# A tanh-shrink polynomial in factored form, its squares and mask on ScalarE, and a shorter weight conversion, in an mLSTM and feed-forward kernel on one core

## The chip, the cores and the metric

One Trainium2 chip, one of its cores. The metric is the device time of one launch in microseconds, as the median of several runs. Engines: TensorE multiplies matrices (PE in the profile, its weight load PEld), VectorE (DVE) and GpSimd (POOL) work elementwise, ScalarE (ACT) evaluates functions, SyncE (SP) issues the loads.

## The reference, cut to what matters

```python
for t in range(S):                                   # q, k, v: (4, 8, 768, 40)
    m_new = np.maximum(f_gate[:, :, t] + m, i_gate[:, :, t])
    f_stab = np.exp(f_gate[:, :, t] + m - m_new); i_stab = np.exp(i_gate[:, :, t] - m_new)
    C = f_stab * C + i_stab * outer(v_t, k_t)
    n = f_stab * n + i_stab * k_t
    y[:, :, t] = sigmoid(o_gate[:, :, t]) * (C @ q_t) / np.maximum(np.abs(n . q_t), 1.0)
...
h = x @ w_in              # x: y as 3072 tokens x 320; w_in: 320 x 2048, float64
g = h - np.tanh(h)        # the "shrink"
out = g @ w_out           # w_out: 2048 x 320, float64
```

Both weight matrices arrive as float64 and the result is float32.

## The kernel before

**Two halves, interleaved.** The recurrence is worked in 24 cell units (6 chunks of 128 tokens for each of 4 batches, 8 heads at once): matmuls for the decay `pd`, the scores `ps`, the products `ph`, `pi`, `pc`, with elementwise work between. Two units make a token group of 256 tokens, transposed into `xT`. The feed-forward part runs over 12 groups g and 8 pairs p of 128-row slices of the 2048 hidden features. For each (g, p), `up` makes six matmuls into one PSUM tile `ph_up` (128 x 512), `shrink` turns it into `gt` in SBUF, and two pairs later (LAG = 2) `down` makes four matmuls with `w_out` into `po`. `ph_up` has two buffers in turn.

**The shrink.** `h - tanh(h)` loses its digits for small h. So for h*h up to 0.1225 (`SMALL`) an odd polynomial in h stands in for it: a degree-9 one in four coefficients (`POLY`) with z = h*h. ScalarE copies h out of PSUM, squares it into z and takes Tanh; GpSimd makes t = h - tanh(h); VectorE makes four polynomial steps into `gt`, a compare of z with `SMALL` in place, and a predicated copy of t over `gt` where z is large (L384 to L394).

**The weights.** `weights` (L167) turns a float64 block into float32 from its two 32-bit words, `hi` and `lo`. It cuts exponent `w_e`, upper mantissa `w_m` and lower mantissa `w_r` out of the words on VectorE (L182, L183, L186, L187), rescales the three on ScalarE (L184, L188, L189), adds and multiplies them on GpSimd (L190, L191) and merges the sign on VectorE (L192). There are 40 blocks: three of `w_in` (128, 128 and 64 rows by 256 columns) and two of `w_out` (128 x 320) for each p. The loads go through four `w64` buffers; `w_e`, `w_m` and `w_r` have two each. Blocks of the first three p are converted beside the first four cell units, the other five p within the first token group, three pairs ahead of their use (EARLY = 3).

**What sets the order.** The code lists work by rough costs and merges cell work with dense work; the tile framework then sets each engine's order and its waits. In the trace every engine works its queue strictly in that order.

Of the kernel before, what the change touches and what calls it, by code (L numbers as in the profile page):

```python
# [25 lines left out]
FP = mybir.dt.float32  # L26
BF = mybir.dt.bfloat16
I32 = mybir.dt.int32
I64 = mybir.dt.int64
AF = mybir.ActivationFunctionType  # L30
OP = mybir.AluOpType
PSUM = bass.MemoryType.PSUM
# [1 line left out]
L = 128  # L34


POLY = (0.333333319193414, -0.13332963338892476, 0.05381595747274004, -0.019838061344260048)
SMALL = 0.35 * 0.35


# [1 line left out]
def kernel(  # L42
# [14 lines left out]
    V, A, G, T = nc.vector, nc.scalar, nc.gpsimd, nc.tensor  # L57

    B, NT, D, H, _ = qT.shape
# [8 lines left out]
    TG = GT * L  # L68
# [3 lines left out]
    LAG = 2  # L72

    const = ctx.enter_context(tc.tile_pool(name="const", bufs=1))
# [3 lines left out]
    mlp = ctx.enter_context(tc.tile_pool(name="mlp", bufs=2))  # L78
# [34 lines left out]
    after = const.tile([128, 128], FP, name="after")  # L113
    bar = const.tile([128, 128], BF, name="bar")
    ones = const.tile([128, D], FP, name="ones")
    make_identity(nc, ident)
    make_identity(nc, ident_b)
    V.memset(ones, 1.0)
# [27 lines left out]
    def to_columns(row):  # L146
        p = ps_b.tile([L, NT, BH], FP, name="pcol", tag="b")
        for c in range(NT):
            T.transpose(p[:, c, :], row[:, c * L:(c + 1) * L], ident[0:BH, 0:BH])
        return p  # L150

    V.tensor_copy(out=lfT, in_=to_columns(lf))
    A.activation(out=eiT, in_=to_columns(i_sb), func=AF.Exp)
    for dst, w in ((eG, upto), (eS, after), (eT, ones)):
        p = ps_b.tile([dst.shape[0], NT, BH], FP, name="psum_lf", tag="b")
        T.matmul(p.rearrange("p c n -> p (c n)"), w, lfT.rearrange("p c n -> p (c n)"),
                 start=True, stop=True)
        A.activation(out=dst, in_=p, func=AF.Exp)

# [7 lines left out]
    def weights(dst, src):  # L167

        p, n = dst.shape
        if src.dtype == FP:  # L170
            nc.sync.dma_start(out=dst, in_=src)
            return
        st = conv.tile([128, n], I64, name="w64", tag="w64", bufs=4)[0:p]
        nc.sync.dma_start(out=st, in_=src)
        words = st.bitcast(I32).rearrange("p (n two) -> p n two", two=2)
        lo, hi = words[:, :, 0], words[:, :, 1]
        e = conv.tile([128, n], I32, name="w_e", tag="w_e")[0:p]
        m = conv.tile([128, n], I32, name="w_m", tag="w_m")[0:p]
        r = conv.tile([128, n], I32, name="w_r", tag="w_r")[0:p]
        mf, rf = m.bitcast(FP), r.bitcast(FP)  # L180

        V.tensor_scalar(out=e, in0=hi, scalar1=20, scalar2=0x7FF, op0=OP.logical_shift_right, op1=OP.bitwise_and)  # L182
        V.tensor_scalar(out=e, in0=e, scalar1=896.0, scalar2=1151.0, op0=OP.max, op1=OP.min)  # L183
        A.activation(out=e, in_=e, func=AF.Copy, scale=float(1 << 23), bias=-896.0 * (1 << 23))  # L184

        V.tensor_single_scalar(m, hi, 0xFFFFF, op=OP.bitwise_and)  # L186
        V.tensor_single_scalar(r, lo, 8, op=OP.logical_shift_right)  # L187
        A.activation(out=mf, in_=m, func=AF.Copy, scale=2.0 ** -20, bias=1.0)  # L188
        A.activation(out=rf, in_=r, func=AF.Copy, scale=2.0 ** -44)  # L189
        G.tensor_tensor(out=rf, in0=rf, in1=mf, op=OP.add)  # L190
        G.tensor_tensor(out=rf, in0=rf, in1=e.bitcast(FP), op=OP.mult)  # L191
        V.scalar_tensor_tensor(out=dst.bitcast(I32), in0=hi, scalar=-(1 << 31), in1=r,  # L192
                               op0=OP.bitwise_and, op1=OP.bitwise_or)
# [3 lines left out]
    def load_w_in(j):  # L197
        cols = slice(j * WB, (j + 1) * WB)
        for c, (r0, rows) in enumerate(KC):
            weights(w_in[0:rows, c, cols], moe_w_in[r0:r0 + rows, cols])  # L200

    def load_w_out(f):
        weights(w_out[:, f, :], moe_w_out[f * 128:(f + 1) * 128, :])
# [31 lines left out]
    def scores(n, half):  # L235
        h4 = slice(half * HH, (half + 1) * HH)

        def decay():
# [6 lines left out]
            t["E"] = att.tile([L, HH, L], FP, name="E", tag="E")  # L245
            A.activation(out=t["E"], in_=pd, func=AF.Exp)  # L246

# [115 lines left out]


    gT, po = {}, {}
    c0, c1, c2, c3 = POLY

    def up(g, p):
        ph = {}

        def product(i, j):
            if not ph:
                ph[0] = ps_h.tile([128, 2, TG], FP, name="ph_up", tag="ph")
            f = 2 * p + i
            T.matmul(ph[0][:, i, :], w_in[:, j, f * 128:(f + 1) * 128], xT[g % 2][:, j, :],  # L375
                     start=(j == 0), stop=(j == NK - 1))
            if (i, j) == (1, NK - 1):
                shrink(ph[0])

        def shrink(ph):  # L380
            h = mlp.tile([128, 2, TG], FP, name="h", tag="h")
            z = mlp.tile([128, 2, TG], FP, name="z", tag="z")
            t = mlp.tile([128, 2, TG], FP, name="t", tag="t")
            A.copy(out=h, in_=ph)  # L384
            A.activation(out=z, in_=ph, func=AF.Square)  # L385
            A.activation(out=t, in_=ph, func=AF.Tanh)  # L386
            G.tensor_tensor(out=t, in0=h, in1=t, op=OP.subtract)  # L387
            gt = gT[g, p] = mlp.tile([128, 2, TG], FP, name="gt", tag="gt", bufs=LAG + 2)
            V.scalar_tensor_tensor(out=gt, in0=z, scalar=c2 / c3, in1=z, op0=OP.add, op1=OP.mult)  # L389
            V.scalar_tensor_tensor(out=gt, in0=gt, scalar=c1 / c3, in1=z, op0=OP.add, op1=OP.mult)  # L390
            V.scalar_tensor_tensor(out=gt, in0=gt, scalar=c0 / c3, in1=z, op0=OP.add, op1=OP.mult)  # L391
            V.scalar_tensor_tensor(out=gt, in0=gt, scalar=c3, in1=h, op0=OP.mult, op1=OP.mult)  # L392
            V.tensor_single_scalar(z, z, SMALL, op=OP.is_gt)  # L393
            V.copy_predicated(gt, z.bitcast(I32), t)  # L394

        return [(0.43, lambda i=i, j=j: product(i, j)) for i in range(2) for j in range(NK)]

# [38 lines left out]
    for x in range(len(pairs) + LAG):  # L436
        g, p = divmod(x, NP)
# [55 lines left out]
```

## Time and profile before

| | |
|---|---|
| median of 3 runs | 795.27 us (794.84 to 796.79) |
| profiled execution | 795.82 us, span 794.1 us |
| TensorE matmul busy | 714.1 us, 90% of the span |
| VectorE busy | 701.9 us, 88%, 1093 instructions |
| ScalarE busy | 249.9 us, 31%, 533 instructions |
| GpSimd busy | 341.5 us, 43%, 333 instructions |
| DMA | 34.93 MB, mean 44 GB/s |

Busy time is the time between an instruction's start and end, so it holds what an instruction waits inside itself. "Idle before, releaser" at a row's end is what the engine waited for ahead of it. The span runs from the first to the last instruction; some 1.7 us of the execution's time lie around it.

### The profile page before, as it was taken

The page shows a single profiled execution, that of the slowest core. Times are in us where ns is not written, and L with a number is a line of the kernel's source. Part 1 is how long each engine was busy: PE and PEld are TensorE (multiplying, and loading weights), DVE is VectorE, ACT ScalarE, POOL GpSimd, SP SyncE. Part 2 cuts the span into 40 slices and gives each one's busy share as a digit, 9 for nine tenths or more (in the row PEclk, how much of TensorE's full clock was granted, in tenths as well). Part 3 has the DMA queues.
Part 4 walks back from the last instruction along what each step waited for, and adds up shares of the span by engine and source line. Part 5 has one row for each costly group of instructions (what it writes and reads, how often), then busy time and mean ns, then how long its engine had stood idle before and what let it go on. Part 6 is the DMA issues. An engine that isn't in the chain of part 4 may idle for free.

```text
span 794.1 us, 10022 instructions
## 1 busy us (share of the span) xinstructions
PE 714.1 (90%) x3562; PEld 549.0 (69%) x3562; DVE 701.9 (88%) x1093; ACT 249.9 (31%) x533; POOL 341.5 (43%) x333
## 2 busy tenths in 40 slices
PE   4655947559999999999999999999999999999996
PEld 2433635327778778777777877877877888787784
DVE  8888887888999889889889889888988998889996
ACT  1442443432322332223223222323223233323332
POOL 7766847664344443433433433433333332222331
PEclk9856996768999999999999999999999999999999
DMA  5344222210110110101111111002101000000000
GB/s 159 92 133 134 82 74 84 75 50 9 51 34 26 41 34 26 50 26 38 38 34 43 34 26 51 26 25 59 42 26 35 24 9 17 1 17 1 0 18 17
DMA packets 21618, 34.93 MB, mean 44 GB/s; under 512 B 2688, under 2 KB 14976, under 8 KB 21568
## 3 DMA queue, kind: packets, MB, share of 16 engines
q1 hardware_dynamic: 18112, 30.35, 13.4%
q10 hardware_dynamic: 3456, 3.93, 1.3%
q8 instruction: 28, 0.46, 0.3%
q14 instruction: 22, 0.18, 0.1%
HBM read 30.34 MB, written 3.93 MB: 43 GB/s over the span
## 4 chain that ended last, share of the span: by engine, by line
PE 61%; DVE 22%; POOL 8%; issue 6%; ACT 2%; DMA 0%; ACTq 0%; DVEq 0%; POOLq 0%
PE ph_up L375 23%; PE po L403 20%; PE ps L253 4%; PE pd L244 4%; POOL w_r L190 3%; PE ph L305 3%; DVE gt L390 3%; POOL w_r L191 2%; PE pi L274 2%; DVE gt L389 2%; DVE gt L392 2%; DVE gt L391 2%; DVE gt L394 2%; PE pc L285 2%; DVE z L393 2%
## 5 line engine op out<-in xcount | busy, mean ns | idle before, releaser
L375 PE MATMUL ph_up<-xT,w_in 128*128 128x256 f32 x1152 | 332.9, 404 | 20.8 <-DVE w_in L192 18.9
L403 PE MATMUL po<-w_out,gt 128*128 128x320 f32 x768 | 269.4, 461 | 9.5 <-DVE gt L394 9.1
L387 POOL TENSOR_TENSOR t<-h,t 128x512 f32<-128x512 f32 x96 | 136.0, 1416 | 295.9 <-ACT t L386 285.6
L375 PEld LDWEIGHTS ph_up<-xT,w_in 128*128 128x128 f32 x1152 | 200.3, 196 | 59.6 <-issue 22.1
L403 PEld LDWEIGHTS po<-w_out,gt 128*128 128x128 f32 x768 | 132.2, 196 | 35.0 <-DVE gt L394 10.8
L384 ACT COPY h<-ph_up 128x512 f32<-128x512 f32 x96 | 56.1, 584 | 223.9 <-PE ph_up L375 141.5
L390 DVE SCALAR_TENSOR_TENSOR gt<-gt,z 128x512 f32<-128x512 f32 x96 | 121.3, 1264 | 2.3
L389 DVE SCALAR_TENSOR_TENSOR gt<-z 128x512 f32<-128x512 f32 x96 | 83.6, 871 | 41.6 <-ACT z L385 41.6
L253 PEld LDWEIGHTS ps<-qT,kT 128*128 128x128 f32 x384 | 69.5, 207 | 36.7 <-ACT E L246 13.8
L253 PE MATMUL ps<-qT,kT 128*128 128x128 f32 x384 | 72.3, 295 | 10.2 <-ACT E L246 6.2
L305 PEld LDWEIGHTS ph<-vw,P 128*128 128x128 f32 x384 | 67.8, 193 | 17.3 <-DVE state L290 1.8
L394 DVE COPY_PREDICATED gt<-z,t 128x512 f32<-128x512 int32 x96 | 75.7, 789 | 2.8
L391 DVE SCALAR_TENSOR_TENSOR gt<-gt,z 128x512 f32<-128x512 f32 x96 | 73.1, 762 | 2.2
L392 DVE SCALAR_TENSOR_TENSOR gt<-gt,h 128x512 f32<-128x512 f32 x96 | 72.3, 753 | 1.3
L274 PEld LDWEIGHTS pi<-state,qT 128*128 128x128 f32 x320 | 61.1, 195 | 17.7 <-ACT xT L343 3.8
L225 POOL TENSOR_TENSOR Vt<-lfT,upto 128x1024 f32<-128x1024 f32 x24 | 46.3, 1929 | 33.2 <-PE pd L244 21.8
L385 ACT ACTIVATE z<-ph_up 128x512 f32<-128x512 f32 x96 | 57.8, 602 | 7.4 <-DVE gt L394 7.4
L305 PE MATMUL ph<-vw,P 128*128 128x41 f32 x384 | 57.5, 249 | 1.4 <-DVE state L290 1.4
L386 ACT ACTIVATE t<-ph_up 128x512 f32<-128x512 f32 x96 | 57.7, 601 | 0.0
L244 PE MATMUL pd<-Vt,after 128*128 128x512 f32 x96 | 54.8, 655 | 0.0
L190 POOL TENSOR_TENSOR w_r<-w_r,w_m 128x256 f32<-128x256 f32 (+2 forms) x40 | 38.3, 957 | 35.7 <-ACT w_r L189 35.7
L274 PE MATMUL pi<-state,qT 128*128 128x41 f32 x320 | 50.6, 245 | 2.9 <-ACT xT L343 2.9
(82 smaller groups left out, 698.0 us busy)
## 6 DMA issues: line engine op xcount, KB each, us to landing
w<-in_moe_w_out SPq DMA_DIRECT2D x16, 320.0 KB
w<-in_moe_w_in SPq DMA_DIRECT2D x16, 256.0 KB
qT<-in_qT SPq DMA_DIRECT2D x24, 160.0 KB
kT<-in_kT SPq DMA_DIRECT2D x24, 160.0 KB
v<-in_v SPq DMA_DIRECT2D x24, 160.0 KB
k<-in_k SPq DMA_DIRECT2D x24, 160.0 KB
o<-in_o_gate SPq DMA_DIRECT2D x24, 160.0 KB
out<-ob ACTq DMA_DIRECT2D x24, 160.0 KB
```

What stands on the lines that cost most here:

```text
L244: T.matmul(pd, after, t["Vt"][:, h4, :], start=False, stop=True)
L253: T.matmul(t["ps"][:, j, :], t["kT"][:, h, :], t["qT"][:, h, :], start=True, stop=True)
L274: T.matmul(t["pi"][:, h, :], t["qT"][:, h, :], old[:, h, :], start=True, stop=True)
L305: T.matmul(t["ph"][:, h, :], t["P"][:, h, :], t["vw"][:, h, :], start=True, stop=True)
L375: T.matmul(ph[0][:, i, :], w_in[:, j, f * 128:(f + 1) * 128], xT[g % 2][:, j, :], start=(j == 0), stop=(j == NK - 1))
L387: G.tensor_tensor(out=t, in0=h, in1=t, op=OP.subtract)
L389: V.scalar_tensor_tensor(out=gt, in0=z, scalar=c2 / c3, in1=z, op0=OP.add, op1=OP.mult)
L390: V.scalar_tensor_tensor(out=gt, in0=gt, scalar=c1 / c3, in1=z, op0=OP.add, op1=OP.mult)
L391: V.scalar_tensor_tensor(out=gt, in0=gt, scalar=c0 / c3, in1=z, op0=OP.add, op1=OP.mult)
L392: V.scalar_tensor_tensor(out=gt, in0=gt, scalar=c3, in1=h, op0=OP.mult, op1=OP.mult)
L394: V.copy_predicated(gt, z.bitcast(I32), t)
L403: T.matmul(po[tt], gT[g, p][:, i, tt * L:(tt + 1) * L], w_out[:, f, :], start=(f == 0), stop=(f == NFF - 1))
```

## The change

The polynomial is written as lead * (z + root) * ((z + c)^2 + rest) * h * z. ScalarE gives z, Tanh, q = (z + c)^2 as a Square with a bias, and the mask `big` as Relu(z - SMALL). VectorE reads h straight from PSUM, in w = (h * lead) * z and in t = h - tanh(h), and no copy of h is made. GpSimd has no part in the shrink. For the weights VectorE masks the exponent bits, shifts the upper mantissa left, and merges the sign; ScalarE rescales, clamps the exponent from below by Relu, and reads the low words itself. GpSimd's two products stay.

```diff
+    V.memset(rebias, -896.0 * (1 << 23))
+    V.memset(square, POLY[2])
+    V.memset(border, -SMALL)
...
-        lo, hi = words[:, :, 0], words[:, :, 1]
+        lo, hi = st.bitcast(U32).rearrange("p (n two) -> p n two", two=2)[:, :, 0], words[:, :, 1]
...
-        V.tensor_scalar(out=e, in0=hi, scalar1=20, scalar2=0x7FF, op0=OP.logical_shift_right, op1=OP.bitwise_and)
-        V.tensor_scalar(out=e, in0=e, scalar1=896.0, scalar2=1151.0, op0=OP.max, op1=OP.min)
-        A.activation(out=e, in_=e, func=AF.Copy, scale=float(1 << 23), bias=-896.0 * (1 << 23))
-
-        V.tensor_single_scalar(m, hi, 0xFFFFF, op=OP.bitwise_and)
-        V.tensor_single_scalar(r, lo, 8, op=OP.logical_shift_right)
-        A.activation(out=mf, in_=m, func=AF.Copy, scale=2.0 ** -20, bias=1.0)
-        A.activation(out=rf, in_=r, func=AF.Copy, scale=2.0 ** -44)
+        V.tensor_single_scalar(e, hi, 0x7FF00000, op=OP.bitwise_and)
+        A.activation(out=e, in_=e, func=AF.Relu, scale=8.0, bias=rebias[0:p])
+
+        V.tensor_single_scalar(m, hi, 12, op=OP.logical_shift_left)
+        A.activation(out=mf, in_=m.bitcast(U32), func=AF.Copy, scale=2.0 ** -32, bias=1.0)
+        A.activation(out=rf, in_=lo, func=AF.Copy, scale=2.0 ** -52)
         G.tensor_tensor(out=rf, in0=rf, in1=mf, op=OP.add)
         G.tensor_tensor(out=rf, in0=rf, in1=e.bitcast(FP), op=OP.mult)
...
-            A.copy(out=h, in_=ph)
             A.activation(out=z, in_=ph, func=AF.Square)
             A.activation(out=t, in_=ph, func=AF.Tanh)
-            G.tensor_tensor(out=t, in0=h, in1=t, op=OP.subtract)
...
-            V.scalar_tensor_tensor(out=gt, in0=z, scalar=c2 / c3, in1=z, op0=OP.add, op1=OP.mult)
-            V.scalar_tensor_tensor(out=gt, in0=gt, scalar=c1 / c3, in1=z, op0=OP.add, op1=OP.mult)
-            V.scalar_tensor_tensor(out=gt, in0=gt, scalar=c0 / c3, in1=z, op0=OP.add, op1=OP.mult)
-            V.scalar_tensor_tensor(out=gt, in0=gt, scalar=c3, in1=h, op0=OP.mult, op1=OP.mult)
-            V.tensor_single_scalar(z, z, SMALL, op=OP.is_gt)
-            V.copy_predicated(gt, z.bitcast(I32), t)
+            A.activation(out=q, in_=z, func=AF.Square, bias=square)
+            A.activation(out=big, in_=z, func=AF.Relu, bias=border)
+            V.scalar_tensor_tensor(out=w, in0=ph, scalar=lead, in1=z, op0=OP.mult, op1=OP.mult)
+            V.tensor_tensor(out=t, in0=ph, in1=t, op=OP.subtract)
+            V.scalar_tensor_tensor(out=w, in0=z, scalar=root, in1=w, op0=OP.add, op1=OP.mult)
+            V.scalar_tensor_tensor(out=gt, in0=q, scalar=rest, in1=w, op0=OP.add, op1=OP.mult)
+            V.copy_predicated(gt, big.bitcast(I32), t)
```

The line numbers grow by 5 to 6 in the changed code (L182 becomes L189, L192 becomes L197, L375 becomes L380). VectorE's order where the first blocks of the seventh pair's weights are converted (a number behind a name marks the buffer: w64_1027, w64_1042 and w64_1057 are the pair's three w_in blocks), before:

```order
L182 TENSOR_SCALAR w_e_1029<-w64_1027 128x256
L394 COPY_PREDICATED gt_1008<-z_1002,t_1003 128x512
L183 TENSOR_SCALAR w_e_1029<-w_e_1029 128x256
L186 TENSOR_SCALAR w_m_1030<-w64_1027 128x256
L187 TENSOR_SCALAR w_r_1031<-w64_1027 128x256
L182 TENSOR_SCALAR w_e_1044<-w64_1042 128x256
L186 TENSOR_SCALAR w_m_1045<-w64_1042 128x256
L183 TENSOR_SCALAR w_e_1044<-w_e_1044 128x256
L187 TENSOR_SCALAR w_r_1046<-w64_1042 128x256
L389 SCALAR_TENSOR_TENSOR gt_1121<-z_1115 128x512
L186 TENSOR_SCALAR w_m_1060<-w64_1057 64x256
L390 SCALAR_TENSOR_TENSOR gt_1121<-gt_1121,z_1115 128x512
```

and now, with w64_976 and w64_989 as its first two:

```order
L192 TENSOR_SCALAR w_m_979<-w64_976 128x256
L396 SCALAR_TENSOR_TENSOR w_1057<-ph_up_1041,z_1053 128x512
L197 SCALAR_TENSOR_TENSOR w_out_173<-w64_905,w_r_909 128x320
L197 SCALAR_TENSOR_TENSOR w_out_173<-w64_918,w_r_922 128x320
L189 TENSOR_SCALAR w_e_978<-w64_976 128x256
L189 TENSOR_SCALAR w_e_991<-w64_989 128x256
L192 TENSOR_SCALAR w_m_992<-w64_989 128x256
L397 TENSOR_TENSOR t_1055<-ph_up_1041,t_1055 128x512
L398 SCALAR_TENSOR_TENSOR w_1057<-z_1053,w_1057 128x512
L197 SCALAR_TENSOR_TENSOR w_in_172<-w64_976,w_r_980 128x256
L399 SCALAR_TENSOR_TENSOR gt_1058<-q_1054,w_1057 128x512
L197 SCALAR_TENSOR_TENSOR w_in_172<-w64_989,w_r_993 128x256
```

Two steps a block instead of four stand ahead of the merges, and the subtraction t stands among them. ScalarE's order at the same place, before:

```order
L385 ACTIVATE z_1248<-ph_up_1219 128x512
L184 ACTIVATE w_e_1029<-w_e_1029 128x256
L188 ACTIVATE w_m_1030<-w_m_1030 128x256
L189 ACTIVATE w_r_1031<-w_r_1031 128x256
L184 ACTIVATE w_e_1044<-w_e_1044 128x256
L188 ACTIVATE w_m_1045<-w_m_1045 128x256
L189 ACTIVATE w_r_1046<-w_r_1046 128x256
L188 ACTIVATE w_m_1060<-w_m_1060 64x256
L386 ACTIVATE t_1249<-ph_up_1219 128x512
L184 ACTIVATE w_e_1059<-w_e_1059 64x256
```

and now:

```order
L392 ACTIVATE z_1177<-ph_up_1149 128x512
L193 ACTIVATE w_m_979<-w_m_979 128x256
L393 ACTIVATE t_1179<-ph_up_1149 128x512
L194 ACTIVATE w_r_980<-w64_976 128x256
L194 ACTIVATE w_r_993<-w64_989 128x256
L190 ACTIVATE w_e_978<-w_e_978,rebias_112 128x256
L190 ACTIVATE w_e_991<-w_e_991,rebias_112 128x256
L193 ACTIVATE w_m_992<-w_m_992 128x256
L394 ACTIVATE q_1178<-z_1177,square_113 128x512
L395 ACTIVATE big_1180<-z_1177,border_114 128x512
L194 ACTIVATE w_r_1006<-w64_1002 64x256
```

The low words' activations come first and read the loaded block, and q and big stand ahead of the next block's.

More of the change, by code (lines that the diff above doesn't have):

```diff
@@ L29 @@
 I64 = mybir.dt.int64
+U32 = mybir.dt.uint32
 AF = mybir.ActivationFunctionType
@@ L34 @@
 L = 128
-POLY = (0.333333319193414, -0.13332963338892476, 0.05381595747274004, -0.019838061344260048)
+POLY = (-0.019838061344260048, -2.6070109206805303, -0.05287600604508702, 6.442407825412434)
 SMALL = 0.35 * 0.35
@@ L115 @@
     ones = const.tile([128, D], FP, name="ones")
+    rebias = const.tile([128, 1], FP, name="rebias")
+    square = const.tile([128, 1], FP, name="square")
+    border = const.tile([128, 1], FP, name="border")
+    V.memset(rebias, -896.0 * (1 << 23))
+    V.memset(square, POLY[2])
+    V.memset(border, -SMALL)
     make_identity(nc, ident)
@@ L365 @@
     gT, po = {}, {}
-    c0, c1, c2, c3 = POLY
+    lead, root, _, rest = POLY
     def up(g, p):
@@ L380, in shrink @@
         def shrink(ph):
-            h = mlp.tile([128, 2, TG], FP, name="h", tag="h")
             z = mlp.tile([128, 2, TG], FP, name="z", tag="z")
+            q = mlp.tile([128, 2, TG], FP, name="q", tag="q")
             t = mlp.tile([128, 2, TG], FP, name="t", tag="t")
-            A.copy(out=h, in_=ph)
+            big = mlp.tile([128, 2, TG], FP, name="big", tag="big")
+            w = mlp.tile([128, 2, TG], FP, name="w", tag="w")
+            gt = gT[g, p] = mlp.tile([128, 2, TG], FP, name="gt", tag="gt", bufs=LAG + 2)
             A.activation(out=z, in_=ph, func=AF.Square)
             A.activation(out=t, in_=ph, func=AF.Tanh)
-            G.tensor_tensor(out=t, in0=h, in1=t, op=OP.subtract)
-            gt = gT[g, p] = mlp.tile([128, 2, TG], FP, name="gt", tag="gt", bufs=LAG + 2)
-            V.scalar_tensor_tensor(out=gt, in0=z, scalar=c2 / c3, in1=z, op0=OP.add, op1=OP.mult)
-            V.scalar_tensor_tensor(out=gt, in0=gt, scalar=c1 / c3, in1=z, op0=OP.add, op1=OP.mult)
-            V.scalar_tensor_tensor(out=gt, in0=gt, scalar=c0 / c3, in1=z, op0=OP.add, op1=OP.mult)
-            V.scalar_tensor_tensor(out=gt, in0=gt, scalar=c3, in1=h, op0=OP.mult, op1=OP.mult)
-            V.tensor_single_scalar(z, z, SMALL, op=OP.is_gt)
-            V.copy_predicated(gt, z.bitcast(I32), t)
+            A.activation(out=q, in_=z, func=AF.Square, bias=square)
[5 more added lines that the diff above has]
+            V.copy_predicated(gt, big.bitcast(I32), t)
         return [(0.43, lambda i=i, j=j: product(i, j)) for i in range(2) for j in range(NK)]
```

## The prediction

> **What bounds the kernel now.** I read the busy time by stretches first, then the chain of waits, then single rows of the timeline. Columns of the stretches: from:to, length, then busy us (x instructions) of TensorE matmul, weight load, VectorE, ScalarE and GpSimd, the granted TensorE clock, DMA share, GB/s.
>
> ```profile
> 13.00:100.00 87.00, 60.47 (x288) 42.13 (x287) 74.84 (x144) 34.69 (x88) 64.12 (x73) 0.76 0.36 107
> 100.00:174.00 74.00, 44.68 (x149) 30.23 (x150) 60.37 (x132) 29.90 (x76) 48.85 (x49) 0.76 0.26 76
> 174.00:188.00 14.00, 10.62 (x39) 7.25 (x38) 11.73 (x18) 2.85 (x6) 4.55 (x4) 0.57 0.00 1
> 188.00:720.00 532.00, 530.13 (x2801) 416.53 (x2801) 480.33 (x702) 158.82 (x319) 197.30 (x170) 1.00 0.11 31
> 720.00:780.00 60.00, 59.16 (x255) 47.23 (x255) 56.87 (x78) 19.90 (x39) 17.23 (x12) 1.00 0.02 6
> 780.00:794.10 14.10, 7.28 (x26) 4.30 (x24) 7.68 (x11) 2.43 (x5) 1.54 (x1) 0.98 0.06 23
> ```
>
> From 188 to 780 us TensorE has work in 589.3 of 592 us at full clock. VectorE is 90% busy there, but nobody waits for it: relief of VectorE in that stretch is worth at most the 2.7 us that TensorE idles. What can move are the first 188 us and the last 14.
>
> In the first stretch the weights are converted. TensorE's rows (start, length) show each of the first token group's later up-projections ending with matmuls that waited for the last converted w_in block:
>
> ```profile
> 115.39 1.99 PE L375 MATMUL ph_up<-xT,w_in 128*128 128x256 f32 x8 [2.83 <-DVE w_in L192]
> 134.10 3.78 PE L375 MATMUL ph_up<-xT,w_in 128*128 128x256 f32 x8 [1.56 <-DVE w_in L192]
> 153.84 3.78 PE L375 MATMUL ph_up<-xT,w_in 128*128 128x256 f32 x8 [3.72 <-DVE w_in L192]
> 170.35 3.78 PE L375 MATMUL ph_up<-xT,w_in 128*128 128x256 f32 x8 [0.64 <-DVE w_in L192]
> 188.02 2.40 PE L375 MATMUL ph_up<-xT,w_in 128*128 128x256 f32 x10
> ```
>
> They end at 117.4, 137.9, 157.6 and 174.1 us: 18.9 us an iteration (five weight blocks, one shrink, a quarter of a cell unit), against 6.7 us an iteration later (592 us over 88). The second group starts at 188.0. If conversion ends sooner by some time, everything after it starts sooner by as much.
>
> What holds conversion is seen in VectorE and GpSimd rows side by side:
>
> ```profile
> 106.39 1.43 POOL L191 TENSOR_TENSOR w_r<-w_r,w_e 128x256 f32<-128x256 f32 x1
> 106.56 0.68 DVE L390 SCALAR_TENSOR_TENSOR gt<-gt,z 128x512 f32<-128x512 f32 x1
> 107.78 0.72 POOL L190 TENSOR_TENSOR w_r<-w_r,w_m 128x256 f32<-128x256 f32 x1
> 108.71 0.81 DVE L182 TENSOR_SCALAR w_e<-w 64x256 int32<-64x256 int32 x1
> 109.33 1.31 POOL L387 TENSOR_TENSOR t<-h,t 128x512 f32<-128x512 f32 x1
> 109.44 1.48 DVE L192 SCALAR_TENSOR_TENSOR w_in<-w,w_r 128x256 int32<-128x256 int32 x1
> ...
> 104.03 0.28 DVE L187 TENSOR_SCALAR w_r<-w 128x256 int32<-128x256 int32 x1
> 104.23 0.28 DVE L182 TENSOR_SCALAR w_e<-w 128x256 int32<-128x256 int32 x1
> 110.84 0.28 DVE L183 TENSOR_SCALAR w_e<-w_e 64x256 int32<-64x256 int32 x1
> 29.60 0.41 DVE L192 SCALAR_TENSOR_TENSOR w_in<-w,w_r 64x256 int32<-64x256 int32 x1
> ...
> 67.28 0.31 DVE L182 TENSOR_SCALAR w_e<-w 128x320 int32<-128x320 int32 x1
> 67.51 0.31 DVE L186 TENSOR_SCALAR w_m<-w 128x320 int32<-128x320 int32 x1
> ...
> 126.06 0.86 POOL L191 TENSOR_TENSOR w_r<-w_r,w_e 128x256 f32<-128x256 f32 x1
> 126.26 0.41 DVE L340 COPY xT<-px 128x256 f32<-128x256 f32 x1
> ...
> L225 POOL TENSOR_TENSOR Vt<-lfT,upto 128x1024 f32<-128x1024 f32 x24 | 46.3, 1929 | 33.2 <-PE pd L244 21.8 <-DVE lfT L152 4.6 <-DVE gt L394 4.5
> ```
>
> With GpSimd idle, a conversion step starts 0.20 us after the one before (0.23 for 320 columns); beside a GpSimd operation it takes 0.81. A GpSimd product of 0.72 takes 1.43 when a VectorE operation came first. So the two engines take turns on SBUF operands; their busy times hold each other's waits twice and can't be read as work. The copy from PSUM at 126.26 ran through beside GpSimd. Check of the turns: a record overlaps the next by 0.08, so an iteration's free turns are GpSimd 9.1 (products of five blocks 6 x 0.72 + 4 x 0.86 = 7.8, t 1.3) and VectorE 9.5 (20 conversion steps 4.3, five merges 1.8, shrink 3.4), and by my estimate 2 for the quarter of a cell unit (Vt alone takes 1.9 a unit). The sum, 20.6, is close to the measured 18.9, so about 0.92 of a turn is path.
>
> **The change part by part.** Columns of the next rows: stretch, length, VectorE busy (x), clock, DMA; in order L182, L183, L186, L187. Below them groups: busy, mean ns.
>
> ```profile
> 0.00:188.00 188.00, 23.31 (x40) 0.76 0.32 93
> 0.00:188.00 188.00, 13.86 (x40) 0.76 0.32 93
> 0.00:188.00 188.00, 17.81 (x40) 0.76 0.32 93
> 0.00:188.00 188.00, 17.98 (x40) 0.76 0.32 93
> ...
> L393 DVE TENSOR_SCALAR z<-z 128x512 f32<-128x512 f32 x96 | 44.1, 459 | 0.0
> L394 DVE COPY_PREDICATED gt<-z,t 128x512 f32<-128x512 int32 x96 | 75.7, 789 | 2.8
> L255 DVE TENSOR_TENSOR P<-ps,E 128x512 f32<-128x512 f32 x48 | 32.6, 680 | 0.0
> L385 ACT ACTIVATE z<-ph_up 128x512 f32<-128x512 f32 x96 | 57.8, 602 | 7.4 <-DVE gt L394 7.4
> ```
>
> Conversion: four single-input steps a block become two (mask, shift), the merge stays. Two steps fewer are 24 x 0.41 + 16 x 0.47 = 17.4 us of turns over 40 blocks. The least this can be worth is nothing (hidden behind GpSimd), the most is the difference in busy time, 73.0 - 40 x 2 x 0.45 = 37 us; I take the turns, since rows free of waits measure them. ScalarE reads the low words itself, every second word; no row shows ScalarE with such a step. VectorE's stepped L187 takes 0.28 like the dense L183, so I take 0.41 as now; at double, 40 x 0.41 = 16 us more lie on ScalarE, 40% busy before 188 us. The first ScalarE operation then waits for the DMA alone.
>
> Shrink: out go the ScalarE copy h, two VectorE steps (one short: L393) and GpSimd's t, in come a ScalarE square and Relu (2 x 0.60, less the copy's 0.58: 0.6 us more) and a subtraction on VectorE, five operations for six. Free turns before: 4 x 0.60 + 0.34 + 0.65 = 3.4 on VectorE plus 1.3 on GpSimd. After: w and t read PSUM, priced by L255 (0.68, no dearer than an SBUF one), and like L340 they should wait for no GpSimd operation; the other three hold 2 x 0.60 + 0.65 = 1.85. So 2.85 us of turns a shrink, 20 us over the seven before 188 us. If PSUM sources took turns too, it is 7 x 1.2 = 8 us less.
> The Trainium skill (SBUF — State Buffer, "Who interferes with whom") says the lock is exclusive and that a VectorE instruction with at most one SBUF input, outside the two-port modes, doesn't contend with GpSimd. That speaks for the first price; L340's row agrees only in part, since it has no SBUF input at all, and no run yet shows w's and t's form. By the rule the sum stays; against it, 768.
>
> The ACT queue: q and big stand ahead of later blocks' activations. At 8 x 0.6 us and 40% busy that is covered by ScalarE's idle time; uncovered, 5 us. The ph_up buffer is now freed by VectorE's subtraction instead of ScalarE's Tanh (a rival below). SP's queue keeps its steps; w64 buffers are still freed by the merge, so loads come earlier with it: 107 GB/s in the first stretch would have to become about 130, below the 157 GB/s of the first 20 us:
>
> ```profile
> 0.00:20.00 20.00, 8.52 (x38) 5.67 (x39) 16.86 (x22) 4.04 (x10) 14.67 (x33) 1.00 0.55 157
> ...
> 780.12 2.32 PE L403 MATMUL po<-w_out,gt 128*128 128x320 f32 x8
> 784.20 2.42 PE L403 MATMUL po<-w_out,gt 128*128 128x320 f32 x8 [1.76 <-DVE gt L394]
> 788.11 2.42 PE L403 MATMUL po<-w_out,gt 128*128 128x320 f32 x8 [1.49 <-DVE gt L394]
> ```
>
> The end: TensorE waits 1.76 + 1.49 for the last two shrinks. After the last up-projection (780.3) the new chain is z, Tanh, then t, w, gt, predicated copy: 1.2 + 4 x 0.65 = 3.8, ready at 784.2; the two earlier down-projections run to 784.4. Both waits go: -3.3 us.
>
> Sum: conversion after 81 us, 25 blocks, 10.9 and shrinks 20, times 0.92: 28.4; the first 15 blocks, 6.5 of turns, half of it path, because cell work and waits for ScalarE share that stretch: 3.3; the end 3.3. Together 35. The profiled execution took 795.8 (span 794.1 and 1.7 around), the median is 795.3: 760.
>
> **The rivals.**
> *The busy time comes off whole.* 37 us of conversion, 9.2 of GpSimd's t (seven times 1.31), the end 3.3: 49.5, so 746. For it: VectorE is 85% busy in the stretch. Against: the turns counted twice.
> *The chain hardly shortens.* The chain of waits from 117.4 to 174.1 us:
>
> ```profile
> by line: POOL w_r L190 18.1%; issue 16.6%; POOL w_r L191 13.7%; DVE w_e L182 10.9%; DVE w_in L192 6.9%; ACT w_e L184 6.1%; DVE w_m L186 5.2%; ACT w_r L189 5.0%; DVE w_e L183 4.0%; DVE z L393 2.5%; DVE gt L394 2.4%; DVE w_out L192 2.3%; ACT
> ```
>
> GpSimd's two products lead it and stay. Only L182 and L183, 14.9% of 56.7 us, go: 2.8 an iteration, 14 over five groups of blocks, and the end: 778. The other steps' waits would then take the place of the removed ones.
> *Slower.* VectorE now frees ph_up. The next use of a buffer is two iterations on; from 720 to 780 us, with hardly any cell work, an iteration (12 + 8 matmul records, of 255 in 60 us) takes 4.7 us, its up-projection some 2.6, so 6.8 us pass between the end of one and the reuse. With VectorE's queue more than that behind, TensorE stalls in each of 88 iterations: at 0.5 us each 44 us, over the 35 gained: 804. Against: five operations of 0.7 fit into 4.7 us.
> *No change.* Something else, such as loads, sets the end of conversion: 795.
>
> **How the numbers follow.** A difference under 0.3% can't be told from none. The sum of turns (750 to 770): 0.59. Busy time whole (740 to 750): 0.17. Chain hardly shorter (770 to 785): 0.17. No change: 0.03. Slower: 0.04. Faster 0.93, same 0.03, slower 0.04. The range reaches to the two priced neighbours, 743 to 779, which leaves out under 2 in 10.
>
> **What would show it.** Second group's first up-projection near 156 instead of 188 us; iterations near 14 us between the waits for w_in; GpSimd products nearer 0.72 and 0.86; the two waits at the end gone; 188 to 780 unchanged in length. Wrong if TensorE then waits for the subtraction, or if w and t take over 1 us beside GpSimd, or if ScalarE's reads of low words take 0.8.

## The result, and the profile after

The changed kernel takes 761.66 us (median; 761.25 to 762.04) against 795.19 us (794.84 to 796.79): a ratio of 0.9575, 95% interval 0.9558 to 0.9591, 33.5 us less. The forecast was 760 us. The sum held; two of its terms were wrong by 6 and 13 us in opposite directions, and a third of nearly 6 us was missing. The runs below separate them. Single executions of one kernel differ by up to 3.6 us, so a stretch read from one profiled execution can lie up to 2.8 us from what the medians give.

The stretches of the changed kernel, cut at the first group's first up-projection, the second group's first one, and the end of the last one (columns as in the prediction: from:to, length, busy us of TensorE matmul, weight load, VectorE, ScalarE, GpSimd, then clock and DMA), and the same cuts of before:

```profile
0.00:77.80 77.80, 48.95 (x225) 33.20 (x225) 58.11 (x97) 29.99 (x71) 58.01 (x83) 0.77 0.43 129
77.80:162.79 84.99, 65.45 (x270) 47.49 (x270) 71.92 (x132) 50.81 (x112) 54.76 (x61) 0.81 0.29 88
162.79:749.40 586.61, 586.61 (x3049) 462.59 (x3048) 415.69 (x688) 242.19 (x442) 93.83 (x94) 1.00 0.10 29
749.40:760.30 10.90, 6.85 (x25) 4.25 (x23) 3.36 (x6) 3.15 (x6) 0.00 (x0) 0.96 0.09 30
```
```profile
0.00:81.25 81.25, 45.77 (x223) 31.50 (x223) 69.37 (x127) 27.61 (x70) 57.08 (x81) 0.77 0.44 128
81.25:188.02 106.77, 71.79 (x266) 49.43 (x265) 87.71 (x178) 41.13 (x101) 68.32 (x70) 0.76 0.22 67
188.02:780.30 592.28, 589.57 (x3056) 464.02 (x3056) 537.48 (x780) 178.70 (x358) 214.53 (x182) 1.00 0.10 29
780.30:794.10 13.80, 6.98 (x24) 4.03 (x23) 7.38 (x11) 2.43 (x5) 1.54 (x1) 0.98 0.06 24
```

The four stretches give back 3.5, 21.8, 5.7 and 2.9 us: 33.8 of the span. In the second stretch VectorE is still the busy engine (85%; in the first it is as busy as GpSimd, 58.1 and 58.0 us); in the third TensorE now shows no idle time at all. The up-projections of the first group, as TensorE's rows show them, no longer end with matmuls that wait for a converted block; three of them start with one that waits for VectorE's subtraction to free `ph_up`, two of these shown:

```profile
113.22 3.30 PE L380 MATMUL ph_up<-xT,w_in 128*128 128x256 f32 x12
126.75 5.09 PE L380 MATMUL ph_up<-xT,w_in 128*128 128x256 f32 x12 [5.21 <-DVE t L397]
141.95 4.33 PE L380 MATMUL ph_up<-xT,w_in 128*128 128x256 f32 x12 [5.81 <-DVE t L397]
162.79 2.84 PE L380 MATMUL ph_up<-xT,w_in 128*128 128x256 f32 x12
...
754.24 2.42 PE L409 MATMUL po<-w_out,gt 128*128 128x320 f32 x8 [0.42 <-DVE gt L400]
```

The last row is the end: of the two waits for the last shrinks one is left, 0.42 us. VectorE and GpSimd side by side:

```profile
119.72 1.89 POOL L230 TENSOR_TENSOR Vt<-lfT,upto 128x1024 f32<-128x1024 f32 x1
119.79 1.97 DVE L192 TENSOR_SCALAR w_m<-w 128x256 int32<-128x256 int32 x1 [0.72 <-POOL w_r L195]
121.57 0.91 POOL L196 TENSOR_TENSOR w_r<-w_r,w_e 128x320 f32<-128x320 f32 x1
121.68 0.68 DVE L396 SCALAR_TENSOR_TENSOR w<-ph_up,z 128x512 f32<-128x512 f32 x1
...
112.20 0.77 POOL L195 TENSOR_TENSOR w_r<-w_r,w_m 128x256 f32<-128x256 f32 x1
112.31 0.68 DVE L397 TENSOR_TENSOR t<-ph_up,t 128x512 f32<-128x512 f32 x1
```

A shift that takes 0.28 us alone is 1.97 us long when GpSimd's `Vt` came first. `w` and `t`, which read one operand from PSUM, take 0.68 us beside a GpSimd operation, and none of their 96 records each is over 0.70. The Trainium skill ("SBUF — State Buffer", "Who interferes with whom": no contention with at most one SBUF input outside the two-port modes) agrees with the two rows. The prediction said that no run showed this form yet; L255 of before has it (`ps` in PSUM, `E` in SBUF), and its 48 records there lie between 0.67 and 0.69 us.

Groups of VectorE in the second stretch (busy, mean ns, idle before), then of GpSimd in the first 163 us, then of ScalarE over the whole span:

```profile
L192 DVE TENSOR_SCALAR w_m<-w 128x320 int32<-128x320 int32 (+2 forms) x23 | 12.3, 534 | 0.9 <-POOL w_r L195 0.9
L197 DVE SCALAR_TENSOR_TENSOR w_in<-w,w_r 128x256 int32<-128x256 int32 (+1 forms) x15 | 9.9, 659 | 7.5 <-POOL w_r L196 7.5
L189 DVE TENSOR_SCALAR w_e<-w 128x320 int32<-128x320 int32 (+2 forms) x23 | 9.9, 432 | 0.0
L197 DVE SCALAR_TENSOR_TENSOR w_out<-w,w_r 128x320 int32<-128x320 int32 x10 | 7.7, 768 | 4.6 <-POOL w_r L196 4.6
...
L195 POOL TENSOR_TENSOR w_r<-w_r,w_m 128x256 f32<-128x256 f32 (+2 forms) x40 | 36.0, 900 | 24.5 <-ACT w_m L193 21.9 <-ACT w_r L194 2.3
L196 POOL TENSOR_TENSOR w_r<-w_r,w_e 128x256 f32<-128x256 f32 (+2 forms) x40 | 34.4, 860 | 5.2 <-ACT w_e L190 2.6
...
L394 ACT ACTIVATE q<-z,square 128x512 f32<-128x512 f32 x96 | 69.3, 722 | 0.0
L395 ACT ACTIVATE big<-z,border 128x512 f32<-128x512 f32 x96 | 69.1, 719 | 0.0
L392 ACT ACTIVATE z<-ph_up 128x512 f32<-128x512 f32 x96 | 57.2, 596 | 208.0 <-PE ph_up L380 206.0 <-DMA out<-ob 1.8
L190 ACT ACTIVATE w_e<-w_e,rebias 128x256 int32<-128x256 int32 (+2 forms) x40 | 20.9, 524 | 13.9 <-DVE w_e L189 13.8
L193 ACT ACTIVATE w_m<-w_m 128x256 f32<-128x256 uint32 (+2 forms) x40 | 17.2, 430 | 9.3 <-DVE w_m L192 9.1
L194 ACT ACTIVATE w_r<-w 128x256 f32<-128x256 uint32 (+2 forms) x40 | 18.1, 452 | 21.3 <-DVE w_out L197 10.9 <-DVE w_in L197 10.1
```

The steps that stay are still long, 0.43 to 0.77 us on average, and VectorE idles 13.0 us there for GpSimd's products.

### The profile page after: what moved, and what is told of

Its sections match the earlier page's. It is cut to its first block, busy times and chain, and to the rows that moved or that the text cites. A ratio compares the mean times of both kernels' runs of the same rounds, so it can differ in the third digit from the quotient of the medians.

```text
span 760.3 us, 9877 instructions
## 1 busy us (share of the span) xinstructions
PE 707.9 (93%) x3562; PEld 547.5 (72%) x3562; DVE 549.1 (72%) x920; ACT 326.1 (43%) x629; POOL 206.6 (27%) x237
## 3 DMA queue, kind: packets, MB, share of 16 engines
q1 hardware_dynamic: 18112, 30.35, 13.5%
## 4 chain that ended last, share of the span: by engine, by line
PE 78%; POOL 10%; DVE 6%; issue 4%; ACT 2%; ACTq 0%; POOLq 0%; DVEq 0%
PE ph_up L380 33%; PE po L409 27%; PE ps L258 4%; PE pd L249 4%; PE ph L310 3%; POOL w_r L195 3%; PE pi L279 3%; POOL w_r L196 3%; PE pc L290 2%; PE px L341 1%; POOL Vt L230 1%; DVE w_m L192 1%; PE pd L248 1%; DVE w_e L189 1%; DVE w_in L197 1%
## 5 line engine op out<-in xcount | busy, mean ns | idle before, releaser
L380 PE MATMUL ph_up<-xT,w_in 128*128 128x256 f32 x1152 | 329.6, 403 | 12.2 <-DVE t L397 11.5
L380 PEld LDWEIGHTS ph_up<-xT,w_in 128*128 128x128 f32 x1152 | 201.2, 196 | 49.9 <-issue 30.1
L396 DVE SCALAR_TENSOR_TENSOR w<-ph_up,z 128x512 f32<-128x512 f32 x96 | 66.2, 689 | 141.3 <-ACT t L393 141.2
L400 DVE COPY_PREDICATED gt<-big,t 128x512 f32<-128x512 int32 x96 | 70.7, 736 | 3.5
L399 DVE SCALAR_TENSOR_TENSOR gt<-q,w 128x512 f32<-128x512 f32 x96 | 70.2, 731 | 3.1
L394 ACT ACTIVATE q<-z,square 128x512 f32<-128x512 f32 x96 | 69.3, 722 | 0.0
L395 ACT ACTIVATE big<-z,border 128x512 f32<-128x512 f32 x96 | 69.1, 719 | 0.0
L398 DVE SCALAR_TENSOR_TENSOR w<-z,w 128x512 f32<-128x512 f32 x96 | 66.3, 691 | 0.0
L397 DVE TENSOR_TENSOR t<-ph_up,t 128x512 f32<-128x512 f32 x96 | 65.2, 679 | 0.0
L233 POOL TENSOR_TENSOR vw<-v,eiT 128x320 f32<-128x320 f32 x24 | 18.2, 760 | 159.6 <-PE ph L310 142.3
L251 ACT ACTIVATE E<-pd 128x512 f32<-128x512 f32 x48 | 28.5, 594 | 70.2 <-PE pd L249 70.2
```

Source lines behind the costliest of these rows:

```text
L394: A.activation(out=q, in_=z, func=AF.Square, bias=square)
L395: A.activation(out=big, in_=z, func=AF.Relu, bias=border)
L396: V.scalar_tensor_tensor(out=w, in0=ph, scalar=lead, in1=z, op0=OP.mult, op1=OP.mult)
L398: V.scalar_tensor_tensor(out=w, in0=z, scalar=root, in1=w, op0=OP.add, op1=OP.mult)
L399: V.scalar_tensor_tensor(out=gt, in0=q, scalar=rest, in1=w, op0=OP.add, op1=OP.mult)
L400: V.copy_predicated(gt, big.bitcast(I32), t)
```

## The experiments

Medians of before in the experiments were 795.15 to 795.57 us. "Start" below is the start of the second group's first up-projection in the profile (162.79 in the changed kernel, 188.02 in before), "first" that of the first group (77.80 and 81.25), and "last" the end of the last up-projection of all (749.5 and 780.3). In some of the kernels two matmul records of the second group's first up-projection run 1.6 us ahead of the other ten; there the start of the ten is taken.

### Each half alone

The kernel before with the new conversion alone, then with the new shrink alone:

```diff
+        V.tensor_single_scalar(e, hi, 0x7FF00000, op=OP.bitwise_and)      # first kernel: conversion new, shrink old
...
+            V.scalar_tensor_tensor(out=w, in0=ph, scalar=lead, in1=z, op0=OP.mult, op1=OP.mult)   # second: shrink new, conversion old
```

> The kernel before with the new weight conversion alone (the shrink stays). Theory of turns (VectorE and GpSimd take turns on SBUF operands): 17.4 us of turns go, 10.9 x 0.92 + 3.3 = 13 us off the start, nothing at the end: about 782 us, second group's first up-projection near 175 us, the two waits at the end (1.8 and 1.5 us) stay. Busy time off whole: 37 us, 758. Chain hardly shorter: below 5 us, 790 or more.

> The kernel before with the new shrink alone (conversion as before). Theory of turns: seven shrinks of 2.85 us of turns before the second group starts, times 0.92, is 18 us; the end gives 3 and the stretch between up to 5: about 770 us. If the gain were the conversion's alone: 787 (end and stretch between only). With the conversion's 13 us this would add up to the whole change's 33.5 us.

Measured: conversion alone 777.05 us (0.9769, 0.9754 to 0.9783), shrink alone 781.61 us (0.9826, 0.9806 to 0.9845). The gains, 18.1 and 13.5 us, sum to 31.6 of 33.5. The second and third stretch of the one, then of the other:

```profile
76.18:168.46 92.28, 67.85 (x267) 48.35 (x265) 78.52 (x133) 45.24 (x102) 69.53 (x70) 0.77 0.26 82
168.46:761.61 593.15, 589.97 (x3056) 463.86 (x3056) 538.71 (x782) 179.27 (x358) 213.99 (x182) 1.00 0.10 29
```
```profile
84.46:183.07 98.61, 64.49 (x267) 47.26 (x267) 82.53 (x181) 47.22 (x109) 55.52 (x63) 0.83 0.24 72
183.07:770.14 587.07, 587.07 (x3053) 463.10 (x3052) 413.97 (x685) 242.76 (x443) 93.94 (x92) 1.00 0.10 29
```

The conversion moves the start by 19.6 us and leaves the rest as it was; the first group's first up-projection starts 5.1 us earlier (76.18). The shrink moves the start by 4.9 us, the middle stretch by 5.2 us and the end by 3.1 us. Ahead of the first up-projection, where no shrink runs, the shrink alone is 3.2 us later than before (84.46 against 81.25), and behind it 8.2 us shorter (98.6 against 106.8). The work ahead of it stands in another order there; what makes it longer was not tested. The conversion came out between the sum of turns (782) and the busy time (758), the shrink between its turns (770) and nothing (787). So the conversion is worth more than was priced, the shrink far less before the start, and more behind it.

### Is it the wait for `ph_up`?

In the shrink alone TensorE waits 24.5 us for the subtraction in the first group. Two kernels put ScalarE's copy of h back, so that ScalarE frees `ph_up` and `w` and `t` read SBUF: the changed kernel so, and the shrink alone so.

```diff
+            A.copy(out=h, in_=ph)
-            V.scalar_tensor_tensor(out=w, in0=ph, scalar=lead, ...
-            V.tensor_tensor(out=t, in0=ph, in1=t, op=OP.subtract)
+            V.scalar_tensor_tensor(out=w, in0=h, scalar=lead, ...
+            V.tensor_tensor(out=t, in0=h, in1=t, op=OP.subtract)
```

> The changed kernel with ScalarE's copy of h back, so that w and t read SBUF and ph_up is freed by ScalarE, not by VectorE's subtraction. If that wait (11.5 us of TensorE in the first group) sets the time: its 11.5 us go, 750 us. If VectorE's turns set it and the wait only shows where they run out: w and t now take turns with GpSimd, up to 8 us more in the first group, 762 to 769 us, and TensorE waits for gt or w_in instead.

> The kernel with the new shrink alone (781.6 us), and ScalarE's copy of the product back, so that the two operations that read the product read the copy and ScalarE sets the product's buffer free. In the shrink alone TensorE waits 24.5 us in the first stage for VectorE's subtraction to free that buffer. If that wait is why the shrink gained only 4.9 us there, up to 10 us come back: 772 to 777. If the weights alone decide and the wait only stands in front of theirs, nothing comes back, and the copy costs what it cost the whole change, 2.7 us: 782 to 784.

Measured: 764.41 us (0.9611, 0.9595 to 0.9627), 2.7 us slower than the change, and 781.43 us (0.9825, 0.981 to 0.984), the same as the shrink alone. TensorE's waits in the shrink alone and in the shrink with the copy:

```profile
PE ph_up L382 <- DVE t L399: 24.5, 6, 9.1
```
```profile
PE ph_up L382 <- DVE w_in L199: 14.9, 6, 5.8
```

The wait for the buffer goes and the wait for the converted block comes in its place, and the time stays the same. In the changed kernel it is the wait for the shrinks' results that grows, from 6.2 to 13.4 us in the first group. All are waits for VectorE's queue; which of its results TensorE meets first matters little. The test isn't clean: with the copy `w` and `t` read SBUF alone, and in the changed kernel their records in the first group grow from 0.67 and 0.68 to 0.77 and 0.82 us, so a gain of 1 or 2 us from the wait's end could be hidden.

### The price of one step

Two, then one more VectorE step in each block, as load only; then one of the removed steps in its real place; then one more 512-word operation in each shrink:

```diff
+        x = conv.tile([128, n], I32, name="w_x", tag="w_x")[0:p]
+        V.tensor_single_scalar(x, hi, 0xFFFFF, op=OP.bitwise_and)          # two: both lines
+        V.tensor_single_scalar(x, hi, 20, op=OP.logical_shift_right)       # one: a shift of the low word instead
...
+        V.tensor_single_scalar(r, words[:, :, 0], 8, op=OP.logical_shift_right)   # in its place
-        A.activation(out=rf, in_=lo, func=AF.Copy, scale=2.0 ** -52)
+        A.activation(out=rf, in_=r, func=AF.Copy, scale=2.0 ** -44)
...
+            V.scalar_tensor_tensor(out=x, in0=z, scalar=root, in1=z, op0=OP.add, op1=OP.mult)     # shrink
```

> The changed kernel with two more VectorE steps in each block of the weight conversion, of the kind that the change removed, into a tile that nothing reads: so two steps are put back as load, without their place in the chain. The conversion alone gained 18.1 us. If a step is worth the turn on the operands that it takes (the prediction's price: 10.9 us of turns after 81 us of the span at 0.92, and 3.3 us before), this costs 13.3 us: 775. If two steps lie on the path with all that the conversion gained, 780. If the gain came from the shorter chain of one block (GpSimd's addition no longer waits for two VectorE steps), the dummies are mostly covered and cost under 6 us: 762 to 768.

> The changed kernel with one more VectorE step in each block of the conversion (the low word's shift, into a tile that nothing reads): the load of the step that stood back in its place in the last kernel of this kind (770.0), without its place in the chain. Two such steps cost 23.2 us. If a step costs its own duration wherever it stands, half of that, 773; if the order in the block counts and the real step's 8.3 us hold more than load, under 768; if the two cost alike, 769 to 771.

> The changed kernel with one of the removed steps back, in its place: VectorE shifts the low word, ScalarE converts the shifted word. If a step is worth its turn, half of the two: 768. If a step is worth what the conversion gained, half of that: 771. If the chain of a block is what counts, it costs more than half of what two dummy steps cost: over 770 with the dummies under 768.

> The changed kernel with one more VectorE operation of 512 words in each shrink, into a tile that nothing reads. Ahead of the second group there are 7 or 8 shrinks. If a step costs its whole record there (0.7 us), 5 us: 767. If it costs its turn (0.3 us), 2 us: 764. In the middle stretch VectorE is busy 71% and idle else; if its load rather than GpSimd's step was what held TensorE there, 1 to 3 us more.

| kernel | us | ratio, 95% | against the change | first | last |
|---|---|---|---|---|---|
| two more steps | 784.85 | 0.9866 (0.985 to 0.9883) | +23.2 | 84.1 | 772.6 |
| one more step | 773.25 | 0.9719 (0.9701 to 0.9737) | +11.6 | 83.1 | 762.7 |
| low-word shift in its place | 769.99 | 0.9682 (0.9667 to 0.9696) | +8.3 | 81.6 | 757.7 |
| one more in each shrink | 769.32 | 0.9672 (0.9655 to 0.9689) | +7.7 | 76.0 | 755.3 |

The dose is linear: 11.6 us for 40 steps, 23.2 for 80, 0.29 us a step, more than any of the three expectations for two steps. The real step costs 8.3 us, 0.21 a step. Behind the first up-projection 25 blocks are left, and there an added step costs (762.7 - 749.5 - 5.3)/25 = 0.32 us, or (772.6 - 749.5 - 6.3)/50 = 0.34 us, and the real one (757.7 - 749.5 - 3.8)/25 = 0.18. These three are rough: the profiled execution of the one-step kernel took 1.9 us more than its median. The turn was priced at 0.20 to 0.23; the records of the added steps, first of the one-step kernel, then of the two-step kernel, are longer:

```profile
L194 DVE TENSOR_SCALAR w_x<-w 128x256 int32<-128x256 int32 (+2 forms) x40 | 15.1, 392 | 0.0
```
```profile
L195 DVE TENSOR_SCALAR w_x<-w 128x256 int32<-128x256 int32 (+2 forms) x40 | 21.9, 552 | 0.1
L194 DVE TENSOR_SCALAR w_x<-w 128x256 int32<-128x256 int32 (+2 forms) x40 | 14.9, 381 | 0.0
```

So an added step's price, 0.29, lies between its turn (0.20 to 0.23) and its record (0.38 to 0.55): part of the wait inside the record would have fallen on the next step, though no run separates this. The real step cost less than the same step as load, about its turn: a longer chain within a block adds nothing here. Why it is 3.3 us less stays open. The step in the shrink costs at least its whole length: 7 records of it before the start, at 0.68 us, are 4.7 us, and the start moved by 5.2, from 162.8 to 168.0; the third stretch grew from 586.6 to 587.3. The medians give 7.7 us, the two profiled executions 5.9. Here is its row:

```profile
L400 DVE SCALAR_TENSOR_TENSOR x_t<-z 128x512 f32<-128x512 f32 x7 | 4.7, 677 | 0.0
```

### GpSimd's step back in the shrink

The changed kernel with the copy of h, and the subtraction on GpSimd:

```diff
-            V.tensor_tensor(out=t, in0=h, in1=t, op=OP.subtract)
+            G.tensor_tensor(out=t, in0=h, in1=t, op=OP.subtract)
```

> The changed kernel with the copy of the product (764.4 us) and the subtraction back on GpSimd: the change without its last part. The shrink alone had gained 4.9 us ahead of the second group and 5.2 us in the middle stretch, 188 to 780 us of before. If the step on GpSimd was the reason, through VectorE's turns after it and results that came late, the middle stretch is again near 592 us and the whole 770 to 776. If VectorE's number of operations was the reason, VectorE has one less here: the middle stretch stays at 587 us and the whole comes to 760 to 766.

Measured: 768.36 us (0.9655, 0.9633 to 0.9677), between the two expectations and 4.0 us above the kernel with the copy alone. The start comes 3.1 us later (167.8 against 164.7), and so does the end of the last up-projection (754.8 against 751.7). The third stretch, 587.0 us, is as long as with the copy alone, and TensorE has no idle time in it:

```profile
167.82:754.80 586.98, 586.98 (x3053) 462.94 (x3052) 451.07 (x597) 285.07 (x531) 201.17 (x181) 1.00 0.10 29
```

So neither GpSimd's step alone nor a sixth VectorE operation alone (587.3 us in the kernel with one more in each shrink) brings TensorE's 2.7 us of idle time back; the old shrink had six operations and GpSimd's step together, which was not run in the new form. The 3.1 us are what GpSimd's step costs over the VectorE operation that it replaces.

### The products on VectorE

The first rival to the turns was that GpSimd's products lead the chain and stay. Three kernels take them off GpSimd: both to VectorE; the first fused with the low word's scaling on VectorE; and both of these.

```diff
-        G.tensor_tensor(out=rf, in0=rf, in1=mf, op=OP.add)
-        G.tensor_tensor(out=rf, in0=rf, in1=e.bitcast(FP), op=OP.mult)
+        V.tensor_tensor(out=rf, in0=rf, in1=mf, op=OP.add)
+        V.tensor_tensor(out=rf, in0=rf, in1=e.bitcast(FP), op=OP.mult)
...
-        A.activation(out=rf, in_=lo, func=AF.Copy, scale=2.0 ** -52)
-        G.tensor_tensor(out=rf, in0=rf, in1=mf, op=OP.add)
+        V.scalar_tensor_tensor(out=rf, in0=lo, scalar=2.0 ** -52, in1=mf, op0=OP.mult, op1=OP.add)   # fused
```

> The changed kernel with the conversion's two products a block on VectorE in place of GpSimd. Theory of turns: GpSimd's 7.8 us of free turns an iteration go, VectorE gets ten operations of 0.33 to 0.40 us, 3.6 us: 4.2 us of turns less, of which VectorE's own queue (then some 13 us an iteration) leaves 1.5: 7 us faster, 754 us, iterations near 13 us. If instead two engines side by side are worth more than fewer turns (products hidden beside VectorE): VectorE's 3.6 us come on top, 5 x 3.6 = 18 us slower, 780 us.

> The changed kernel with the low word scaled and added by one VectorE operation, in place of ScalarE's conversion of it and GpSimd's addition: VectorE 4 steps a block, GpSimd one, ScalarE two. With both products on VectorE the time was 746.6. If GpSimd's products are dear because VectorE and GpSimd take turns, taking away one of two brings about half: 753 to 755. If VectorE's fourth step costs what a step costs in the other direction (6 to 9 us) and GpSimd's addition was hidden, 768 to 771.

> Both products of the conversion on VectorE (746.6 us) and ScalarE's conversion of the low word fused into the first of them: VectorE five steps as there, ScalarE two instead of three, GpSimd none. If VectorE's load alone sets the length of the first group there, no change: 745 to 748. If its waits for ScalarE (3 us for each of two lines in that stretch) lie on the path, 741 to 744.

Measured: 746.64 us (0.9393, 0.9372 to 0.9415), 758.40 us (0.9529, 0.9508 to 0.955) and 753.05 us (0.9467, 0.945 to 0.9485). The first beats both kernels: 15.0 us under the change, with 80 more operations on the engine that was already the bound. Its first stretches, and VectorE's groups in the second:

```profile
0.00:70.50 70.50, 44.41 (x221) 30.58 (x222) 62.20 (x124) 29.33 (x68) 33.84 (x51) 0.78 0.49 148
70.50:150.10 79.60, 61.90 (x274) 45.82 (x272) 76.22 (x186) 50.92 (x113) 13.12 (x13) 0.85 0.29 89
```
```profile
L195 DVE TENSOR_TENSOR w_r<-w_r,w_m 128x256 f32<-128x256 f32 (+2 forms) x25 | 11.3, 456 | 3.2 <-ACT w_m L193 3.2
L196 DVE TENSOR_TENSOR w_r<-w_r,w_e 128x256 f32<-128x256 f32 (+2 forms) x25 | 11.0, 445 | 0.0
L189 DVE TENSOR_SCALAR w_e<-w 128x320 int32<-128x320 int32 (+2 forms) x24 | 8.7, 362 | 0.2 <-DMA w<-in_moe_w_out 0.2
L192 DVE TENSOR_SCALAR w_m<-w 128x256 int32<-128x256 int32 (+2 forms) x25 | 7.4, 296 | 0.0
L197 DVE SCALAR_TENSOR_TENSOR w_in<-w,w_r 128x256 int32<-128x256 int32 (+1 forms) x15 | 6.0, 409 | 0.0
```

The two products take 22.3 us there. Against the change, the shift falls from 0.534 to 0.296 us, the mask from 0.432 to 0.362, the w_in merge from 0.659 to 0.409, and the 13.0 us of idle time before the merges and the shift are gone; VectorE is 96% busy. Up to the start (150.1 against 162.8) VectorE's busy time grows by only 8.4 us, although the 80 products take 38.8 of it, and its idle time falls by 21.1. So what the products on GpSimd cost VectorE in waits, inside its records and between them, was more than the products on VectorE itself. How much of it is turns, and how much the handovers between the engines within a block, no run separates. The forecast of 754 had seen half of the gain.

Fusing brought less than half (758.4, expected 753 to 755) when one product stayed on GpSimd, and lost 6.4 us when none did, where no change or a small gain was expected. VectorE's two products in that last kernel, first 150 us, against 0.474 and 0.501 us before fusing:

```profile
L195 DVE TENSOR_TENSOR w_r<-w_r,w_e 128x256 f32<-128x256 f32 (+2 forms) x40 | 21.9, 553 | 0.0
L194 DVE SCALAR_TENSOR_TENSOR w_r<-w,w_m 128x256 f32<-128x256 uint32 (+2 forms) x40 | 20.5, 517 | 2.6 <-ACT w_m L193 2.4
```

They are 40 x (0.052 + 0.043) = 3.8 us longer. The two profiled spans, 751.4 and 747.6 us, lie 3.8 us apart too, but the medians 6.4, so this may be part of the loss only. Why both products became longer stays open. ScalarE's saved operation bought nothing.

## Why the prediction was right, and which of its terms were not

**The stage.** That VectorE's queue in the first 188 us is what conversion, and so everything behind it, runs by, was right: the time follows the number of VectorE steps linearly (11.6 us for one step a block, 23.2 for two), and hardly follows which wait TensorE shows. VectorE's waits for GpSimd are part of that queue: with 80 operations more, but GpSimd's products gone, the kernel was 15.0 us faster.

**Conversion, priced 10.0 + 3.3 = 13.3 us: 18.1 measured in the conversion alone, 19.6 at the start.** The mis-sized term is the price of a step: the factors 0.92 and a half made 13.3 us of 17.4 us of turns, and the steps cost all of their turns or a little more. Behind the first up-projection 10.0 us were priced and 14.5 measured (19.6 less 5.1), over the 10.9 us of turns: 0.29 us a step for a turn of 0.22. Ahead of it 3.3 were priced and 5.1 measured. Cut at the end of the group's second up-projection (85.7 us against 88.8 in before), the parts are 16.5 and 3.1 us, so the split is known to some 2 us only. The steps' records fell from 73.0 to 41.0 us, by far more than the kernel gained, so the caution against reading busy time as work held:

```profile
L185 DVE TENSOR_SCALAR w_e<-w 128x256 int32<-128x256 int32 (+2 forms) x40 | 20.5, 513 | 0.2 <-DMA w<-in_moe_w_in 0.2
L188 DVE TENSOR_SCALAR w_m<-w 128x256 int32<-128x256 int32 (+2 forms) x40 | 20.5, 512 | 1.8 <-POOL w_r L191 1.8
```

**Shrinks before the start, 20 x 0.92 = 18.4 us: 4.9 measured**, 8.2 behind the first up-projection less the 3.2 by which that came later. The failed step is "the other three hold 2 x 0.60 + 0.65": `w` and `t` were given no turn, since they don't contend with GpSimd. They don't, and that part held; but each still fills VectorE's own queue, as the added operation did (5.2 us for seven). That one reads SBUF, so for an operand in PSUM this is an inference. At 0.60 us each, `w` and `t` take 7 x 1.2 x 0.92 = 7.7 us off: 10.7 would have been the price, against 8.2. The rest stays open. GpSimd's `t`, priced 1.3 us each, 9.1 in all, was not the error: the run that put it back lost 3.1 us although VectorE had one operation less, and if that operation was worth 5.2 us, GpSimd's `t` was worth about 8. Turns for `w` and `t` too, priced 8 us, showed as 2.7 us with both reading SBUF, net of what the end of the wait for `ph_up` may have given back.

**The middle, priced at nothing, bounded by 2.7 us: 5.7 measured.** TensorE's 2.7 us of idle time went, with the shrink alone. The other 3.0 us are inside matmul records at a granted clock of 1.00 in both; 7 records more in before's stretch make 1.3 of them, and 1.7 are open. The bound, "relief of VectorE in that stretch is worth at most the 2.7 us that TensorE idles", counted TensorE's idle time alone, and didn't hold.

**The end, 3.3 us: 2.9.** One wait went, of the other 0.42 us is left. Behind Tanh VectorE has five operations, not the four that were priced: `w` too starts only after Tanh, at 750.67, and the predicated copy ends at 754.19.

So 13.3 + 18.4 + 3.3 = 35 stood against 19.6 + 4.9 + 5.7 + 2.9 = 33, and the sum was right by errors that cancel: the time was hit partly by luck. Of what was to show it, the iterations came (14.2 us between the starts of the first group's last up-projections, 99.09 to 155.94, forecast near 14). The second group starts at 163, forecast 156. GpSimd's products, forecast nearer 0.72 and 0.86, stayed at 0.90 and 0.86 on average (0.96 and 0.90 before). The middle did change in length, and one sign of being wrong did come: TensorE waits for the subtraction.

**ScalarE.** Its stepped read of the low words takes 0.45 us on average against 0.43 for the dense L193: right. "The first ScalarE operation then waits for the DMA alone" was wrong: it waits 21.0 us for the merge, which frees one of the two buffers of `w_r`. More buffers weren't tried. `q` and `big`, priced 0.60, take 0.72: 11.5 us each over 96 on an engine with room.

**The rivals.** The wait of the slower rival appeared (11.5 us in the first group, none in the 587 us behind it), and neither kernel with the copy, where it is gone, is faster. The busy time did not come off whole: the conversion brought 18.1 of 37 us. The chain that hardly shortens had the right leader and the wrong end: the changed kernel's chain from 101.8 to 159.7 us is still led by GpSimd's two products, with the shares that they had.

```profile
by line: POOL w_r L195 18.1%; POOL w_r L196 14.3%; issue 12.1%; DVE w_m L192 6.9%; DVE w_e L189 6.8%; DVE w_out L197 5.2%; PE ph_up L380 5.0%; DVE w_in L197 4.3%; ACT w_m L193 3.6%; DVE o L271 3.6%; DVE t L397 3.3%; POOL Vt L230 3.2%; DVE w
```

## What to carry to other kernels

On an in-order engine that is full, give every operation a price, whether or not it contends. A step that takes turns with another engine cost between its free interval and its record here (0.21 us as the real step, 0.29 as a dummy, with records of 0.34 to 0.55); a dummy step in one and two doses measures it in two runs. Where a chain is led by operations of a second engine that takes turns with the full one, moving them onto the full engine can be the better change: here it was worth 15 us more. And which wait the consumer shows is no guide when all its waits are for one queue. Where terms are added up, test each alone: a sum that comes out says little of its terms.

## What was not expected of the hardware

An elementwise operation with two SBUF inputs on GpSimd (0.86 to 0.90 us on average) cost the kernel more than the same operation put on a VectorE that was 85% busy (0.45 us). A VectorE operation with one operand in PSUM ran at 0.68 us beside GpSimd's, where one of the same shape with SBUF operands alone took up to 1.7 us (L390 of before). An activation with its bias in a tile was longer than one of the same shapes with a constant: 0.52 us (L190) against 0.43 (L184 of before, on the same tile). The function differs too, Relu for Copy, and no run separates the two.
